# Three moves in a fused attention and MLP kernel: the output weight's casts in the last group, one subtraction block in the first group, and the places where x is added in memory

## The chip, the cores and the metric

The kernel runs on one core of one Trainium2 chip. The metric is the device time of one execution in microseconds (us). The time before is the median of three runs. One further execution was profiled; all instruction rows below come from it.

## What is computed

x has 2048 tokens of 576 features. All arithmetic is in f32.

```python
xn = layernorm(x)
A  = sliding_dilated_attention(xn @ wqkv) @ wo       # 32 heads of 18, 8 keys, 2 apart
h  = gelu(layernorm(x) @ w1)                         # 576 x 576
x1 = x + shift_quarters(h) @ w2                      # token shifts +1, -1, +2, -2
B  = x1 + gelu(layernorm(x1) @ w3) @ w4              # w3: 576 x 4608, w4: 4608 x 576
out = x + A + B
```

## The kernel before: tiles, groups and queues

**Split operands.** TensorE multiplies f32 data that was first rounded to its fast f32 form. So every operand is kept as a rounded high part and the low part that is left. ScalarE (ACT) writes the high part as a cast and VectorE (DVE) the low part as a subtraction. `split_w` (L199 to L201) does this for a weight: L200 is the cast on ACT, L201 the subtraction on DVE. Both engines take their instructions strictly in program order.

**Stages.** The kernel first computes q, k and v and keeps them in DRAM, then the token mixing (w1, w2) that gives x1, then the large MLP, and at the end the product with `wo` over 16 tiles of 128 tokens (L1431, L1437), which adds into the sum in `Y` and stores each tile. The attention itself runs on DVE, in slices between other work, during the MLP.

**The MLP's second part** is what the change touches. It has 24 groups, q = 0 to 23: groups 0 to 11 handle one half of the tokens (sb = 0, tiles 0 to 7 of the output), groups 12 to 23 the other half (sb = 1, tiles 8 to 15), both with the same 12 pairs of w3 columns. A group forms its hidden blocks from seven block products, P1 to P7, each of seven matmuls (L1130), in which sums and differences of the blocks of w3 and x take the place of an eighth product. Between the products stand the eight "downs" D0 to D7 (L868, twelve matmuls each) that multiply the *previous* group's hidden blocks with w4. Group 23 is followed by its own eight downs alone, and then by the `wo` tiles.

**Order.** TensorE's order in a group is written out by hand as a string (`ORDER`). At each item a small table, filled by `at(item, function)`, says which other work is issued right after that item:

```python
ORDER = "P1 D0 P2 P6 D1 P5 D2 P7 D3 P4 D4 P3 D5 D6 D7"
ORDERS = {0: "P1 P2 D0 P6 P5 P7 D1 D2 P4 D3 P3", ...}
```

**Names that the steps use:**
- `keep` (L1136) copies a product from PSUM on ACT; `z_add` (L1140) adds another product to it on DVE. In P7, `keep` empties the accumulator on which P4 goes on, so P4 waits for it.
- `gelu12` (L820, L821) and `low12` (L826) make the hidden block c12 out of P3's result: two gelus on ACT, then the low part on DVE. D0 of the next group multiplies c12.
- `combine` (L965) makes four sums and differences of the raw w3 block of the next group, on DVE. `split_s` (L970, L972 on ACT, L976 on DVE, L992, a small accumulating DMA on GpSimd's queue) then splits the result; the next group's P6 is its first reader. `split_a` uses L970 to L983 in the same manner for the blocks that need no combination.
- A down is read out of PSUM by ACT (L873 or L876). PSUM has two buffers for downs, so the down after next waits for it; for some tiles ACT also seeds the next buffer (L849).
- For the ten tiles in `YD = (1, 2, 3, 5, 7, 9, 10, 11, 13, 15)` the output sum lies in DRAM (`yd`). ACT copies the down into a staging slot and GpSimd (POOL) issues a DMA that accumulates it (L874). The final `+ x` is done for them by one more accumulating DMA each, `load_xa` (L886). The order in which POOL issues is the order of its queue; an accumulation on a tile waits until the one before it on that tile has landed.
- `load_wo` (L1166, L206) fetches the five row blocks of `wo` at the start of group 23, from SyncE's (SP's) queue; `split_wo(k)` splits block k into `Wo`. `read_xo` (L174) fetches the attention output behind it, `split_x` (L181 to L188) splits that, and `load_y` (L1392) fetches the `yd` sums at the end.
- `load_pair` (L954, L957) fetches the raw w3 block of a later group.

Of the kernel before, what the change touches and what calls it, by code (L numbers as in the profile page):

```python
# [33 lines left out]
YD = (1, 2, 3, 5, 7, 9, 10, 11, 13, 15)  # L34
# [3 lines left out]
NWP = NF // 2 - NPL  # L38
# [19 lines left out]
def fused_block(ctx, tc, x, wqkv, wo, w1, w2, w3, w4, out):  # L58
# [448 lines left out]
    for b in range(NB):  # L507
        for i, m in enumerate((0, 1, 2, 4, 3) if b < 3 else (4, 0, 1, 2, 3)):
# [12 lines left out]
            k = {(0, 4): 0, (1, 1): 1, (1, 4): 2, (2, 1): 3, (2, 4): 4}.get((b, i))  # L521
# [102 lines left out]
    for t in range(NT):  # L624
# [19 lines left out]
        if t in (4, 5):  # L644
            r0, c0, n = ((256, 128, 128), (HF + 256, 0, 256))[t - 4]
# [8 lines left out]
        if t in (9, 10, 13, 14):  # L654
            k = {9: 4, 10: 6, 13: 8, 14: 10}[t]
# [168 lines left out]
    def low_part(h, g):  # L824
        spent[0] += 0.69
        dve.tensor_tensor(h[:, 1, :], g, h[:, 0, :].bitcast(F32), op=ALU.subtract)  # L826
# [182 lines left out]
    for u, (c, b) in enumerate(units):  # L1009
# [77 lines left out]
        k = u % 4  # L1087
# [107 lines left out]
    for q in range(NQ):  # L1195
        sb = q // NWP
# [28 lines left out]
        low12 = lambda: low_part(hid[q, "c12"], Z2)  # L1225
        n = q + 1
        plan = {}

        def at(it, f, *args):
            plan.setdefault(it, []).append(lambda: f(*args))  # L1230

        if q == 0:
            at("P6", split_op, 0, "T4")
            at("D1", gelu22)
            at("P7", split_a, n, (0, 1))
            at("D1", split_op, 0, "B22")
            at("D1", split_a, n, (2,))
            at("D2", low22)
            at("P4", combine, n)
            at("P3", gelu12)  # L1240
            at("P3", split_s, n, (0, 1))
            at("P3", low12)
            at("P3", split_s, n, (2,))
            at("P3", load_pair, q + 2)
        elif q == NWP - 1:
            rtemps[:] = [2, 13]
            at("P1", load_w4, p, 1)
            for it, k in zip(("P1", "P2", "P6", "P5", "P7", "P4", "P3"),
                             ("B11", "B21", "T2", "T1", "T3", "T4", "B22")):
                at(it, get_op, 1, k)  # L1250
            at("P4", split_w4, p)
            at("P3", split_op, 1, "B11", 0)
            at("D2", split_op, 1, "B11", 1)
            at("D3", gelu22)
            at("D4", low22)
            at("D4", split_op, 1, "B21", 0)
            at("D5", gelu12)
            at("D5", split_op, 1, "B21", 1)
            at("D6", low12)
            at("D6", split_op, 1, "T2", 0)  # L1260
            at("D7", split_op, 1, "T2", 1)
        elif q == NWP:
            rtemps[:] = [2]
            at("D0", split_op, 1, "T1", 0)
            at("D1", split_op, 1, "T1", 1)
            at("P1", split_op, 1, "T3", 0)
            at("D2", split_op, 1, "T3", 1)
            at("P2", split_op, 1, "T4", 0)
            at("P6", split_op, 1, "T4", 1)
            at("D3", split_op, 1, "B22", 0)  # L1270
            at("P5", split_op, 1, "B22", 1)
            at("P5", split_a, n, (0, 1))
            at("P7", split_a, n, (2,))
            at("P7", combine, n)
            at("D4", gelu22)
            at("P4", low22)
            at("D5", gelu12)
            at("D5", split_s, n, (0, 1))
            at("D6", low12)
            at("D6", split_s, n, (2,))  # L1280
            at("D7", load_pair, q + 2)
        elif z < -1:
            at("P1", load_w4, p, 1)
            at("P5" if q < NWP else "D2", split_a, n, (0, 1))
            at("D2" if q < NWP else "P7", split_a, n, (2,))
            at("D3", combine, n)
            at("P4", gelu22)
            at("D4", split_w4, p, 0)
            at("D4", low22)
            at("D5", split_w4, p, 1)  # L1290
            at("P3", split_s, n, (0, 1))
            at("D5", gelu12)
            at("D5", split_s, n, (2,))
            at("D6", low12)
            if z < -2:
                at("D6", load_pair, q + 2 + (q == NWP - 2))
        else:
            at("D3", split_w4, p)
            at("P4", gelu22)
            at("D4", low22)  # L1300
            at("D5", gelu12)
            at("D6", low12)
            for k, it in enumerate(("D1", "P5", "D2", "P7", "D4")):
                at(it, split_wo, k)
        if -5 <= z <= -2:
            for i, (it, nx) in enumerate((("P6", "D1"), ("P7", "D3"), ("P3", "D5"), ("D6", "D7"))):
# [6 lines left out]
            at("D5" if q else "P3", load_w4, NPL + pair(q + 1), 0)  # L1313
        if 0 < q < 9:
            at("D6", sums, 1, q - 1)
        if 0 < q <= len(YD):
            at("D7", load_xa, YD[q - 1])
        if -4 <= z < -1:
            at("P1", put_o, z + 4)
        if z == -2:  # L1320
# [149 lines left out]
```

## Time and profile before

| | us |
|---|---|
| median of 3 runs | 1285.62 (1284.66 to 1286.82) |
| the profiled execution | 1286.14 |
| span of its instructions | 1284.3 |
| TensorE (PE) busy | 1263.6 |
| VectorE (DVE) busy | 900.2 |
| ScalarE (ACT) busy | 721.2 |
| GpSimd (POOL) busy | 252.8 |
| mean granted TensorE clock | 0.994 |

The span runs from the first to the last instruction; 1.84 us of the profiled execution lie around it. In timeline rows the columns are: start, duration, engine, line, operation, output<-input, shapes, count, and in brackets how long the engine had been idle and what released it. PEld is TensorE's weight load. SPq and POOLq rows are a queue's issues. Rows of a stretch give, for each engine, busy us and instruction count, then the granted TensorE clock (1 is full), the DMA engines' busy share and GB/s.

### The profile page before, as it was taken

The numbers are of one execution on the slowest core, as the hardware profiler recorded it, in microseconds if no ns is written. First come the engines' busy times: TensorE is split into PE (matmuls) and PEld (weight loads), VectorE is DVE, ScalarE is ACT, GpSimd is POOL, SyncE is SP. The second block draws the span as 40 slices with busy tenths as digits, with TensorE's granted clock in tenths as the row PEclk, the third lists the DMA queues.
The fourth block names the chain that finished last, engine by engine and source line by source line (L and its number), as shares of the span: only waits on it lengthen the run. The fifth ranks groups of instructions, "written<-read, shape, count | busy, mean of one in ns | idle before, by whom it ended". The sixth has DMA issues, their size and how long they took to land.

```text
span 1284.3 us, 19963 instructions
## 1 busy us (share of the span) xinstructions
PE 1263.6 (98%) x7510; PEld 1158.5 (90%) x7510; DVE 900.2 (70%) x1203; ACT 721.2 (56%) x1155; POOL 252.8 (20%) x366
## 2 busy tenths in 40 slices
PE   9999999999999999999899999999999999999799
PEld 8999998899898989999799999999888988999798
DVE  6455534778558989997659898899889973653341
ACT  3332125526645645455767768776677776775630
POOL 2011100021222111111222232232122222222100
PEclk9999999999999999999999999999999999999899
DMA  7646784246888986859679998899867678899872
GB/s 206 154 123 138 168 175 140 83 130 195 204 224 188 220 167 125 176 117 242 119 166 192 206 189 193 205 187 227 217 126 149 125 147 174 180 219 222 212 239 84
DMA packets 203800, 223.25 MB, mean 174 GB/s; under 512 B 79528, under 2 KB 139528, under 8 KB 203576
## 3 DMA queue, kind: packets, MB, share of 16 engines
q1 hardware_dynamic: 170952, 155.18, 42.4%
q0 software_dynamic: 32752, 66.80, 32.6%
q8 instruction: 59, 0.97, 0.3%
q14 instruction: 37, 0.30, 0.1%
HBM read 124.47 MB, written 107.87 MB: 181 GB/s over the span
## 4 chain that ended last, share of the span: by engine, by line
PE 60%; DMA 4%; ACT 3%; DVE 2%; issue 1%; SPq 1%; DVEq 0%; ACTq 0%; POOLq 0%
PE ps L868 29%; PE cc L1130 17%; PE p L832 10%; PE ps L215 4%; DMA w3st<-in_B_w_dram 1%; DMA x1n<-xn 1%; DMA xt<-xn 1%; DMA wr<-in_A_wo_dram 1%; DMA xt<-td1T 0%; SPq L169 0%; DMA x1n<-td1T 0%; DVE xt L597 0%; DVE w3st L965 0%; SPq L1178 0%; ACT Y L873 0%
## 5 line engine op out<-in xcount | busy, mean ns | idle before, releaser
L868 PEld LDWEIGHTS ps<-w,c 128*128 128x128 f32 x3456 | 477.5, 189 | 23.0 <-ACT c L820 3.5
L868 PE MATMUL ps<-w,c 128*128 128x288 f32 x3456 | 488.8, 295 | 6.3 <-ACT c L820 3.1
L874 POOL DMA_DIRECT2D yd<-Y x154 | 139.3, 908 | 388.2 <-ACT Y L873 330.9
L826 DVE TENSOR_TENSOR c<-Y,c 128x512 fp32r<-128x512 f32 x144 | 98.8, 687 | 93.0 <-ACT Y L815 88.0
L873 ACT COPY Y<-ps 128x576 f32<-128x576 f32 x154 | 97.9, 636 | 74.7 <-PE ps L868 62.0
L215 PE MATMUL ps<-WQ,xt 128*128 128x432 f32 x672 | 134.8, 360 | 0.0
L215 PEld LDWEIGHTS ps<-WQ,xt 128*128 128x128 f32 x672 | 125.6, 188 | 5.7
L1130 PE MATMUL cc<-xt,w3s 128*128 128x512 f32 (+1 forms) x504 | 128.0, 394 | 1.0 <-DVE Y L1140 1.0
L1130 PEld LDWEIGHTS cc<-xt,w3s 128*128 128x128 f32 (+1 forms) x504 | 92.3, 188 | 19.2 <-DVE Y L1140 1.4
L876 ACT COPY Y<-ps 128x576 f32<-128x576 f32 x92 | 58.9, 640 | 65.7 <-PE ps L868 64.3
L1130 PE MATMUL cc<-x1n,w3a 128*128 128x512 f32 (+1 forms) x336 | 86.1, 395 | 0.1
L746 DVE TENSOR_TENSOR po<-q,k 128x1152 f32<-128x1152 f32 (+1 forms) x48 | 84.2, 1755 | 0.8
L749 DVE TENSOR_REDUCE L<-po 128x64 f32<-128x1152 f32 (+1 forms) x48 | 84.0, 1751 | 0.8
L122 POOL TENSOR_TENSOR rs<-rs,mhalf 128x1 f32<-128x1 f32 x48 | 30.8, 643 | 258.0 <-DVE rs L121 147.9
L324 ACT COPY stg<-ps 128x864 f32<-128x864 f32 x24 | 21.2, 882 | 102.7 <-PE ps L215 60.4
L814 ACT ACTIVATE c<-p 128x512 fp32r<-128x512 f32 x48 | 28.6, 596 | 85.8 <-PE p L832 85.8
L722 DVE TENSOR_TENSOR po<-v,L 128x1152 f32<-128x1152 f32 x56 | 75.4, 1354 | 0.9
L1140 DVE TENSOR_TENSOR Y<-cc,Y 128x512 f32<-128x512 f32 x49 | 33.7, 687 | 53.5 <-ACT Y L1136 48.7
L1130 PEld LDWEIGHTS cc<-x1n,w3a 128*128 128x128 f32 (+1 forms) x336 | 60.7, 189 | 11.4 <-DVE w3a L976 0.4
L726 DVE TENSOR_TENSOR po<-po 128x1152 f32<-128x1152 f32 x49 | 66.4, 1355 | 0.9
L849 ACT COPY ps<-Y 128x576 f32<-128x576 f32 x92 | 59.4, 646 | 4.4 <-DVE Y L879 2.4
L215 PE MATMUL ps<-W,h 128*128 128x288 f32 x384 | 53.5, 295 | 0.0
(192 smaller groups left out, 1956.0 us busy)
## 6 DMA issues: line engine op xcount, KB each, us to landing
yd<-Y POOLq DMA_DIRECT2D x156, 288.0 KB, 6.0
Y<-in_B_w_dram SPq DMA_DIRECT2D x29, 576.0 KB, 6.0
w3st<-in_B_w_dram SPq DMA_DIRECT2D x56, 256.0 KB, 7.8
qkvd<-stg SPq DMA_DIRECT2D x24, 432.0 KB, 3.8
yd<-ev POOLq DMA_DIRECT2D x26, 288.0 KB, 7.1
w3st<-in_B_w_dram SPq DMA_DIRECT2D x92, 64.0 KB, 7.3
xd<-st SPq DMA_DIRECT2D x16, 320.0 KB, 6.1
xd<-big SPq DMA_DIRECT2D x16, 320.0 KB, 6.5
```

Of the source, the lines that this page charges most:

```text
L215: pe.matmul(ps[:, h, :n], xs(a), ws(b, h), start=i == 0, stop=i == len(PAIRS) - 1)
L722: dve.tensor_tensor(dst, vv, Lf[:, :, w:w + 1].to_broadcast([128, TPP * GH, HD]), op=ALU.mult)
L726: dve.tensor_tensor(o, o, dst, op=ALU.add)
L746: dve.tensor_tensor(dst, qf[:, None, :].to_broadcast([128, n, TPP * GC]), win, op=ALU.mult)
L749: dve.tensor_reduce(Lw[:, w:w + n, :], dst.rearrange("p w (x d) -> p w x d", d=HD), axis=AX.X, op=ALU.add)
L826: dve.tensor_tensor(h[:, 1, :], g, h[:, 0, :].bitcast(F32), op=ALU.subtract)
L832: pe.matmul(ps, W3[f][:, w, :], x1n[b][:, a, :], start=n == 0, stop=n == len(PAIRS) - 1)
L849: act.copy(ps[:, :, :HF], halves(t))
L868: pe.matmul(ps[:, k, :HF], h[:, col], w[:, p, k * HF:(k + 1) * HF], start=n == 0 and not seed, stop=n == len(seq) - 1, skip_group_check=True)
L873: act.copy(e.rearrange("p (h c) -> p h c", h=2), ps[:, :, :HF])
L874: pool.dma_start(yd[t], e, accum_op=ALU.add)
L1130: pe.matmul(ps, WX[w][:k, v, SLOT[w], :], area[sb][xk][:k, a, :], start=onto is None and i == 0, stop=last and i == len(HALVES) - 1, skip_ ...
```

## The change

```diff
         if q == 0:
...
             at("D2", low22)
-            at("P4", combine, n)
             at("P3", gelu12)
+            at("P3", combine, n)
+            at("P3", low12)
             at("P3", split_s, n, (0, 1))
-            at("P3", low12)
             at("P3", split_s, n, (2,))
...
             at("D6", low12)
-            for k, it in enumerate(("D1", "P5", "D2", "P7", "D4")):
+            for k, it in enumerate(("P4", "D4", "P3", "D5", "D6")):
                 at(it, split_wo, k)
...
-        if 0 < q <= len(YD):
-            at("D7", load_xa, YD[q - 1])
+        if 0 < q - sb * NWP <= 5:
+            at("D7", load_xa, YD[5 - 5 * sb + q - sb * NWP - 1])
```

**First group (q = 0).** `combine` goes from behind P4 to behind P3 and its `z_add`. These are DVE's rows around the end of group 0, before; `cc` is a product, `c` a hidden block, `w3st` the raw w3 block:

```order
L826 TENSOR_TENSOR c_5906<-Y,c_5906 128x512
L965 TENSOR_TENSOR w3st<-w3st 128x3x128 x4
L1140 TENSOR_TENSOR Y<-cc_5866,Y 128x512
L826 TENSOR_TENSOR c_5965<-Y,c_5965 128x512
L976 TENSOR_TENSOR w3s<-w3st,w3s 128x1024
```

And the same place on DVE now:

```order
L826 TENSOR_TENSOR c_5906<-Y,c_5906 128x512
L1140 TENSOR_TENSOR Y<-cc_5866,Y 128x512
L965 TENSOR_TENSOR w3st<-w3st 128x3x128 x4
L826 TENSOR_TENSOR c_5961<-Y,c_5961 128x512
L976 TENSOR_TENSOR w3s<-w3st,w3s 128x1024
```

The four subtractions and additions of L965 have changed places with the addition of L1140. They still stand ahead of c12's low part (the second L826) and of `split_s`.

**Last group (q = 23).** The five casts of `wo` leave the items D1, P5, D2, P7 and D4 and go to P4, D4, P3, D5 and D6. These are ACT's rows from D1's copy on, before:

```order
L873 COPY Y<-ps_11148 128x576
L200 CAST Wo<-wr 128x576 x2
L876 COPY Y<-ps_11199 128x576
L849 COPY ps_11266<-Y 128x2x288
L200 CAST Wo<-wr 128x576
L1136 COPY Y<-cc_11172 128x512
L200 CAST Wo<-wr 128x576
L873 COPY Y<-ps_11236 128x576
L569 CAST w_11149<-Y 128x2x576
L820 ACTIVATE c_11305<-Y 128x512
L821 ACTIVATE Y<-Y 128x512
L876 COPY Y<-ps_11266 128x576
```

ACT's rows now, from the same copy on:

```order
L873 COPY Y<-ps_11148 128x576
L876 COPY Y<-ps_11199 128x576
L849 COPY ps_11262<-Y 128x2x288
L1136 COPY Y<-cc_11172 128x512
L873 COPY Y<-ps_11236 128x576
L569 CAST w_11149<-Y 128x2x576
L820 ACTIVATE c_11297<-Y 128x512
L821 ACTIVATE Y<-Y 128x512
L200 CAST Wo<-wr 128x576
L876 COPY Y<-ps_11262 128x576
L200 CAST Wo<-wr 128x576 x2
L873 COPY Y<-ps_11287 128x576
```

P7's `keep` (L1136) had three casts between itself and D1's copy, and now has none; the first cast stands eight rows later. The fourth cast now stands behind `gelu12`, and the fifth behind the seed (L849) for the first down of the last eight. DVE's L201 rows move along.

**x added in memory.** Before, groups 1 to 10 each added x to one tile of `YD` in its order; that is tiles 1, 2, 3, 5, 7 in groups 1 to 5, while these groups' own downs accumulate on the same tiles, and 9, 10, 11, 13, 15 in groups 6 to 10. Now groups 1 to 5 add x to tiles 9, 10, 11, 13, 15, groups 6 to 10 to none, and groups 13 to 17 to tiles 1, 2, 3, 5, 7. On POOL's queue, around the downs of groups 13 and 14, these rows stand now (the number behind `yd` is the tile):

```order
L874 DMA yd9_92<-Y_71 128x576
L874 DMA yd10_93<-Y_71 128x576
L874 DMA yd11_94<-Y_71 128x576
L886 DMA yd1_87<-in_A_x_dram 128x576
L874 DMA yd13_95<-Y_71 128x576
L983 DMA w3a_9097<-w3t_86 32x384
L874 DMA yd15_96<-Y_71 128x576
```

Before, the same stretch of the queue had no L886 row:

```order
L874 DMA yd9_92<-Y_71 128x576
L874 DMA yd10_93<-Y_71 128x576
L874 DMA yd11_94<-Y_71 128x576
L874 DMA yd13_95<-Y_71 128x576
L983 DMA w3a_9101<-w3t_86 32x384
L874 DMA yd15_96<-Y_71 128x576
```

So one accumulating DMA has come in behind the eighth down, ahead of the next group's first staged tile. The count of instructions is the same on every engine.

## The prediction

> **What bounds the kernel now.** The page first: which engine is nearest to the whole span?
>
> ```profile
> span 1284.3 us, 19963 instructions
> PE 1263.6 (98%) x7510; PEld 1158.5 (90%) x7510; DVE 900.2 (70%) x1203; ACT 721.2 (56%) x1155; POOL 252.8 (20%) x366
> ```
>
> TensorE is idle for 1284.3 - 1263.6 = 20.7 us. The change removes no matmul, so it can only win idle time, and time in which TensorE runs at a low clock. Next, TensorE's waits, longest first, and two rows of the view by stretches:
>
> ```profile
> PE cc L1130 <- ACT Y L1136: 6.9, 2, 6.6
> PE ps L868 <- ACT c L820: 3.1, 1, 3.1
> ...
> 935.00:1160.00 225.00, 225.00 (x1342) 203.26 (x1341) 156.88 (x193) 158.59 (x251) 54.50 (x64) 1.00 0.80 165
> 1160.00:1220.00 60.00, 52.50 (x317) 48.12 (x316) 23.01 (x33) 37.61 (x60) 11.30 (x14) 0.91 0.91 209
> ```
>
> One wait of 6.6 us (a product for the copy of L1136) and one of 3.1 us (a down for the gelu of L820) make half of the idle time. From 935 to 1160 us TensorE has no idle time at all; in the 60 us from 1160 it loses 7.5 us, and its granted clock sinks to 0.91. The change works in both waits, so I read their stretches in the timeline and the chain of waits.
>
> **The last group.** Rows of the timeline and, for the load, the units of 1.59 and 1.62 us and the last line, of the chain:
>
> ```profile
> 1141.73 1.59 PE ps L868 x12
> 1143.32 1.62 PE cc L1130 x7
> ...
> 1183.81 7.50 DMA wr<-in_A_wo_dram
> ...
> 1185.09 1.78 PE L1130 MATMUL cc<-x1n,w3s 128*128 128x512 f32 x7
> ...
> 1191.41 1.28 ACT L200 CAST Wo<-wr 128x576 fp32r<-128x576 f32 x2 [8.69 <-DMA wr<-in_A_wo_dram]
> 1195.04 3.35 PE L1130 MATMUL cc<-xt,w3a 128*128 128x512 f32 x7 [6.58 <-ACT Y L1136]
> 1204.55 0.64 ACT L873 COPY Y<-ps 128x576 f32<-128x576 f32 x1 [2.03 <-PE ps L868]
> 1206.94 0.64 ACT L849 COPY ps<-Y 128x576 f32<-128x576 f32 x1
> 1207.64 4.92 PEld L868 LDWEIGHTS ps<-w,c 128*128 128x128 f32 x36 [0.19 <-ACT ps L849]
> 1209.58 0.64 ACT L876 COPY Y<-ps 128x576 f32<-128x576 f32 x1 [0.23 <-PE ps L868]
> 1213.04 0.63 ACT L873 COPY Y<-ps 128x576 f32<-128x576 f32 x1
> 1213.72 8.20 PE ps L868 x60
> ```
>
> The reader is to see a queue blocked by a load. The first block of `wo` lands at 1183.81 + 7.50 = 1191.31. Its cast (L200, 1191.41) stands on ACT right behind D1's copy. Behind it stand D2's copy, the seed, and L1136, for which P4 waits. So P4 starts at 1195.04.
>
> *P4 without the casts ahead.* P7 starts at 1185.09, D3 behind it; P4 can start at 1185.09 + 1.62 + 1.59 = 1188.30, which is 6.74 us earlier. L1136 is free to run at P7's end, 1186.87, since nothing on ACT is then waiting for memory.
>
> *From P4 to the fourth of the last eight downs.* Before, this stretch is 1213.72 - 1195.04 = 18.68 us. It holds two products and seven downs, at full clock 2 x 1.62 + 7 x 1.59 = 14.37 us. The other 4.31 us are half clock (P4 took 3.35 us instead of 1.62, and the down behind it was slow too) and short waits for ACT. With the idle time gone the clock has no reason to fall, but ACT now has the casts in this stretch, and I count them. The first cast comes at about 1191.4, behind `gelu22`, when its block has just landed; D4's copy stands behind it and has until 1194.7. D5's copy can start at P4 + 1.62 + 1.59 + 1.62 + 1.75 = 1194.9. From D5's copy to the seed of the last eight's first down ACT takes 1206.94 - 1204.55 = 2.39 us; the fourth cast adds 1.28 / 2 = 0.64, so the seed starts at 1197.95 and the down 0.70 later (1207.64 - 1206.94), at 1198.65. TensorE would be ready at 1188.30 + 2 x 1.62 + 4 x 1.59 = 1197.90: 0.75 us lost. The fifth cast and two gelus delay this down's copy by about 0.2 us, to 1200.6. From that copy to the fourth down the first part of `split_x` stands on ACT, as before: 1213.72 - 1209.58 = 4.14. So the fourth down starts at 1204.7 instead of 1213.72. **Term 1: -9.0 us.** From there the instructions and their order are as before; the casts are over by 1199.1 and their DVE parts soon after, more than 12 us ahead of the first `wo` tile.
>
> **The first group.** Timeline rows from c22's low part to P6 of group 1, with the landing time of all L992 DMAs below, and TensorE's clock in one of those microseconds:
>
> ```profile
> 634.00 2.33 DVE L965 TENSOR_TENSOR w3st<-w3st 128x384 f32<-128x384 f32 x4
> 636.25 0.68 DVE L1140 TENSOR_TENSOR Y<-cc,Y 128x512 f32<-128x512 f32 x1
> 637.65 1.04 PE L868 MATMUL ps<-w,c 128*128 128x288 f32 x4 [3.11 <-ACT c L820]
> 638.17 1.03 ACT L970 CAST w3s<-w3st 128x1024 fp32r<-128x1024 f32 x1
> 638.29 0.69 DVE L826 TENSOR_TENSOR c<-Y,c 128x512 fp32r<-128x512 f32 x1 [1.36 <-ACT Y L821]
> 639.04 2.29 PE L868 MATMUL ps<-w,c 128*128 128x288 f32 x8 [0.35 <-DVE c L826]
> 640.12 0.77 POOL L992 DMA_DIRECT2D w3s<-w3st  x1 [4.12 <-ACT w3s L972]
> 642.66 0.42 PEld L1130 LDWEIGHTS cc<-xt,w3s 128*128 128x128 f32 x2
> ...
> DMA to landing us min/median/max: 2.4/2.5/5.2
> ...
> 639.00:640.00 1.00, 0.96 (x4) 0.96 (x5) 0.77 (x1) 1.00 (x3) 0.00 (x0) 0.50 0.08 16
> ```
>
> With the places exchanged, L1140 starts at 634.00, 2.25 us earlier, and D0 can begin 637.65 - 2.25 = 635.40. But c12's low part (L826) still stands behind L965, which now ends at about 634.00 + 0.68 + 2.25 = 636.93 (the lengths from start to start): the low part goes from 638.29 to 636.95, 1.34 us earlier, and D0 halts for it after four matmuls. `split_s` (L970) also needs L965: 638.17 becomes 636.97, 1.2 us earlier, and with it L992's DMA: 640.12 becomes 638.92. Before, that DMA (2.5 us) landed at 642.6 and P6 read it at 642.66, with no slack. So P6 moves by 1.2 us, however early D0 is. **Term 2: -1.2 us** (bounds: -0.8, if TensorE stays at half clock and is itself late for P6; -1.9, the most that D0 and P2 allow).
>
> The row of 639 us shows half clock after a wait of 3.1 us. The Trainium skill ("TensorE: Matmul & The Clock Gate", "Part 1: The HAM clock gate") says that the clock is halved after an idle window of about 3.4 us. By that rule two gaps of 0.9 and 1.0 us with work between keep full clock; by the row, where less sufficed, part of the half clock may stay, which is the end at -0.8.
>
> **x added elsewhere.** Rows: POOL's waits, two rows of group 7, two of group 14, then the landing times of w3's blocks (L954) before and after 880 us, and of the x adds:
>
> ```profile
> POOL yd L886 <- DMA yd<-Y: 10.2, 2, 7.3
> ...
> 818.34 0.84 ACT L970 CAST w3a<-w3st 128x768 fp32r<-128x768 f32 x1 [2.98 <-DMA w3st<-in_B_w_dram]
> 821.45 1.87 PE L1130 MATMUL cc<-xt,w3a 128*128 128x512 f32 x7 [0.35 <-ACT Y L1136]
> 980.45 0.90 SPq L954 DMA_DIRECT2D w3st<-in_B_w_dram  x2
> 992.19 0.83 ACT L970 CAST w3a<-w3st 128x768 fp32r<-128x768 f32 x1
> ...
> DMA to landing us min/median/max: 2.7/7.6/11.3
> ...
> DMA to landing us min/median/max: 5.8/8.5/9.5
> ...
> DMA to landing us min/median/max: 4.0/6.2/9.7
> ```
>
> In groups 1 to 5 the adds waited on POOL for the tile's own accumulation, 10.2 us in two of them. TensorE had no idle time there, so their end is worth nothing: the staging slots hide it. Groups 6 to 10 lose an add each. One stall lies there: in group 7 a w3 block landed late, ACT waited 2.98 us and P4 0.35, and P4 ran 0.24 us long (1.86 is its length after a wait, 1.62 without). Without the add beside that load I take the stall as gone: **-0.6** (bounds 0 and -1.5, since the transition at 870 to 935 us has 2 us of idle time, mostly DVE's). Groups 13 to 17 gain an add each. There a w3 block is issued at 980.45 and used at 992.19: 11.7 us, against landings of at most 9.5 without adds and of 11.3 in the first half with them. No stall would follow; I charge **+0.3** (bounds 0 and +3).
>
> **Sum.** -9.0 - 1.2 - 0.6 + 0.3 = -10.5 us. The profiled execution took 1286.14, so 1275.6; the median of the runs, 0.52 below it, would give 1275.1. I take 1275.4.
>
> **Rivals.**
>
> *The tail becomes memory's (slower than forecast, still faster than before).*
>
> ```profile
> 1208.77 0.87 POOL L874 DMA_DIRECT2D yd<-Y  x1 [0.57 <-ACT Y L873]
> 1216.22 1.24 SPq L174 DMA_DIRECT2D x1n<-xd  x2
> 1233.88 0.75 DVE L1431 TENSOR_TENSOR Y<-ps,Y 128x576 f32<-128x576 f32 x1
> 1236.55 14.97 PE L215 MATMUL ps<-Wo,xt 128*128 128x288 f32 x112
> ```
>
> The third block of the attention output is fetched at 1216.22, when the accumulation issued at 1208.77 has landed (`load_y` waits for its slot). The second `wo` tile's addition waits on DVE behind that block's split, at 1233.88, and the fifth tile (1236.55) needs the buffer that it frees: 1.9 us of slack. When TensorE is 9 us earlier, the accumulations of D5 to D7 fall among the reads of the first two blocks, and may land 2 to 4 us later than their new places ask for. That takes 0 to 3 us back: 1276 to 1279. For it speaks the small slack; against it that the loads are all started by TensorE's progress and so move along.
>
> *The casts still wait (the change does not do what it says).* If the `wo` blocks land 4 us later than 1191.3, the first cast holds D4's copy, which has 2 to 3 us to spare. This gives back the rest and adds short waits: 1277 to 1281. Nothing in the change delays these loads.
>
> *The added x adds starve groups 13 to 17 (slower than before).* Place: the w3 block of the next group, whose cast stands on ACT ahead of the copy that P4 waits for. Price: five times the lateness. It decides from 10.5 / 5 = 2.1 us per group, a landing 13.8 us after issue, since 11.7 are allowed; at 3 us each the time is 1275.4 + 15 = 1290. The add takes 6.2 us; sharing all engines evenly it could add some 3 us to a landing of 9.5, which gives 0.8 us a group, 1279 in all. Against more speaks the first half: with adds and other accumulations no load took over 11.3 us. The Trainium skill ("DMA: Bandwidth & Descriptors", "Queues, rings and completion order") says that each DMA engine takes turns between the queues that have work, packet by packet. By that rule an add can stretch a load by its own 6.2 us at most, to 15.7, 4 us late in each group and 1295.
>
> **Chances.** Forecast (1273 to 1278) 0.66; memory in the tail (to 1280) 0.18; casts that wait 0.06; starved groups, slower than before, 0.05; a mixture that ends near the old time, 0.05, of which I put 0.03 within 0.2% (2.6 us, about what a measurement of this kernel can tell from no change) and 0.02 above. So faster 0.90, same 0.03, slower 0.07. The range: at the low end all favourable bounds, -9.2 - 1.9 - 1.5 = -12.6 from 1285.6, 1273.0; at the high end 3 us given back in the tail, -0.8 in the first group and +1.5 in groups 13 to 17, net -5.3, 1280.5.
>
> **What would show it.** In the changed profile: P4 of the last group at P7 + 3.2 us with no wait for L1136, and no half clock there. A wait of under 1 us at the first and about 1.2 us at the fourth of the last eight downs. In group 1, two short waits of D0 in place of one, P6 1.2 us earlier. No wait in group 7, and L970 in groups 13 to 17 not released by a DMA. I am wrong if the tail of L215 has new waits for L1431, or if casts L200 are released by `wr` at a time when copies stand behind them.

## The result, and the profile after

The changed kernel took 1276.7 us (median of 6 runs, 1275.16 to 1279.68) against 1285.45 us for the kernel before, measured beside it (6 runs, 1284.66 to 1286.82): ratio 0.9935, 95% interval 0.9919 to 0.995. That is faster by about 8.4 us, more than the 0.2% that can be told from no change. It was run twice more, with medians of 1275.63 and 1275.67; over all 17 runs the median is also 1275.63. The forecast was 1275.4.

The profiled execution of the changed kernel is the slowest of its first six, 1279.68 us. Its page begins:

```profile
span 1277.8 us, 19971 instructions
PE 1261.6 (99%) x7510; PEld 1155.8 (90%) x7510; DVE 900.3 (70%) x1203; ACT 722.2 (57%) x1155; POOL 253.0 (20%) x366
```

TensorE's idle time is 1277.8 - 1261.6 = 16.2 us, 4.5 less than before. The span is 6.5 us shorter, though, and TensorE's busy time fell by 2.0 us with the same 7510 matmuls: that part is half clock that has gone. Where the idle time is now, longest waits first (in us: total, times, longest):

```profile
PE ps L868 <- ACT Y L873: 2.1, 2, 1.2
PE ps L868 <- DVE c L826: 1.4, 1, 1.4
...
PE cc L1130 <- ACT cc L1333: 1.4, 2, 1.1
...
PE ps L868 <- ACT c L820: 0.9, 1, 0.9
```

The wait of 6.6 us for L1136 and that of 3.1 us for L820 are both gone. What is left are short waits for low parts (L826), for the copy of a product that stands behind `split_s` on ACT (L1333), for gelus and for copies. The stretches, with the granted clock and the DMA share behind the engines' busy times:

```profile
935.00:1160.00 225.00, 224.99 (x1341) 203.13 (x1340) 157.57 (x193) 160.06 (x255) 59.00 (x69) 1.00 0.83 169
1162.00:1222.00 60.00, 58.08 (x381) 54.21 (x381) 26.80 (x37) 41.98 (x66) 13.75 (x16) 1.00 0.98 241
```

In groups 13 to 21 TensorE still has no idle time, with the five x adds of groups 13 to 17 among them (POOL has 69 rows instead of 64). The last 60 us before the `wo` tiles lose 1.9 us of TensorE instead of 7.5, at full clock instead of 0.91. Now the last group in the timeline of the changed kernel, from P7 to the fourth of the last eight downs:

```profile
1187.43 1.79 PE L1130 MATMUL cc<-x1n,w3s 128*128 128x512 f32 x7
1189.25 0.59 ACT L1136 COPY Y<-cc 128x512 f32<-128x512 f32 x1 [0.25 <-PE cc L1130]
1190.64 1.79 PE L1130 MATMUL cc<-xt,w3a 128*128 128x512 f32 x7
...
1194.56 0.68 ACT L200 CAST Wo<-wr 128x576 fp32r<-128x576 f32 x1 [0.82 <-DMA wr<-in_A_wo_dram]
1195.67 1.25 ACT L200 CAST Wo<-wr 128x576 fp32r<-128x576 f32 x2
1199.13 0.66 ACT L200 CAST Wo<-wr 128x576 fp32r<-128x576 f32 x1
1200.36 0.64 ACT L849 COPY ps<-Y 128x576 f32<-128x576 f32 x1
1201.05 5.19 PE L868 MATMUL ps<-w,c 128*128 128x288 f32 x36 [0.65 <-ACT ps L849]
1207.16 1.06 PE L868 MATMUL ps<-w,c 128*128 128x288 f32 x6 [0.92 <-ACT Y L873]
```

L1136 runs right at P7's end, and P4 starts 1190.64 - 1187.43 = 3.21 us after P7 with no wait. The first cast still waits 0.82 us for its block, but a copy behind it has time to spare. Two waits remain, 0.65 us for the seed of the first of the last eight downs and 0.92 us for a copy ahead of the fourth.

To compare executions whose starts differ, I use the time between the starts of the same TensorE matmuls, from the PE rows of each profile: G1 is group 1 from the last matmul of its first product (P1) to the first of D1; G8 is group 8 from P7 to the end of P4, the place of the stall that the prediction puts in group 7 (counted from q = 0, as in `ORDERS`, P7 at 817.7 us of the kernel before belongs to group 8); G13-21 lies between the same two matmuls near 934 and 1152 us, from group 13 into group 22; T1 runs from P7 to P4 of the last group, T2 from P4 to D5, T3 from D5 to the fourth of the last eight downs, T4 from there to the first `wo` tile. All in us:

| kernel profiled | G1 | G8 | G13-21 | T1 | T2 | T3 | T4 |
|---|---|---|---|---|---|---|---|
| before | 10.37 | 5.43 | 217.55 | 9.95 | 7.72 | 10.96 | 8.03 |
| changed (first profile) | 9.99 | 4.84 | 217.71 | 3.21 | 4.84 | 11.68 | 8.04 |
| changed (after_again) | 9.62 | 4.84 | 217.73 | 3.21 | 4.84 | 11.55 | 8.03 |
| changed (after_side) | 8.40 | 4.84 | 217.75 | 3.21 | 4.84 | 11.56 | 8.04 |
| casts_only | 11.63 | 4.93 | 217.65 | 3.21 | 4.84 | 11.55 | 8.03 |
| combine_only | 8.41 | 5.68 | 217.56 | 12.01 | 6.61 | 10.96 | 8.03 |
| adds_only | 10.62 | 4.84 | 217.56 | 10.16 | 6.36 | 10.95 | 8.03 |
| no_adds | 9.28 | 5.66 | 217.55 | 3.21 | 4.84 | 11.55 | 8.03 |
| first_at_D2 | 9.35 | 4.84 | 217.60 | 6.95 | 6.46 | 11.54 | 8.03 |
| first_at_P7 | 8.41 | 4.84 | 217.54 | 3.21 | 4.84 | 13.55 | 8.03 |
| low_first | 13.24 | 4.84 | 217.54 | 3.21 | 4.84 | 11.55 | 8.03 |
| last_two_later | 9.23 | 4.84 | 218.58 | 3.21 | 4.84 | 11.09 | 8.04 |
| last_two_side | 10.65 | 4.84 | 217.55 | 3.21 | 4.84 | 10.96 | 8.03 |
| split_spread | 9.47 | 4.84 | 217.55 | 3.21 | 4.84 | 11.15 | 8.61 |

T1 to T3 together fell from 28.63 to 19.73 us in the first profile, 8.9 us, G8 by 0.6, and G1 by 0.4 there and by 2.0 in another. The theory is the prediction's: the casts are the main term, because of what stood behind them on ACT's queue, not because of their work. The rivals to tell apart: the gain comes in part from the other two edits; or the casts' ACT time is what counts, wherever they stand; or a wait moves to the `wo` tiles.

### The profile page after: what moved, and what is told of

The parts are those of the page before. It is cut to its first block, busy times and chain, and to the rows that moved or that the text cites. A ratio compares the mean times of both kernels' runs of the same rounds, so it can differ in the third digit from the quotient of the medians.

```text
span 1277.8 us, 19971 instructions
## 1 busy us (share of the span) xinstructions
PE 1261.6 (99%) x7510; PEld 1155.8 (90%) x7510; DVE 900.3 (70%) x1203; ACT 722.2 (57%) x1155; POOL 253.0 (20%) x366
## 4 chain that ended last, share of the span: by engine, by line
PE 63%; DMA 3%; ACT 2%; DVE 2%; issue 1%; SPq 0%; DVEq 0%; ACTq 0%
PE ps L868 30%; PE cc L1130 19%; PE p L832 10%; PE ps L215 4%; DMA w3st<-in_B_w_dram 1%; DMA xt<-xn 1%; DVE w3st L965 1%; DMA x1n<-td1T 0%; DVE xt L597 0%; SPq L1178 0%; DMA Y<-od 0%; PE p L1437 0%; ACT Y L873 0%; ACT xt L927 0%; DVE w3a L976 0%
## 5 line engine op out<-in xcount | busy, mean ns | idle before, releaser
L826 DVE TENSOR_TENSOR c<-Y,c 128x512 fp32r<-128x512 f32 x144 | 98.8, 687 | 88.9 <-ACT Y L815 87.4
L873 ACT COPY Y<-ps 128x576 f32<-128x576 f32 x154 | 98.1, 637 | 75.2 <-PE ps L868 61.7
L876 ACT COPY Y<-ps 128x576 f32<-128x576 f32 x92 | 59.0, 641 | 65.6 <-PE ps L868 64.2
L814 ACT ACTIVATE c<-p 128x512 fp32r<-128x512 f32 x48 | 28.7, 599 | 85.7 <-PE p L832 85.7
L1140 DVE TENSOR_TENSOR Y<-cc,Y 128x512 f32<-128x512 f32 x49 | 33.7, 688 | 59.9 <-ACT Y L1136 55.1
L849 ACT COPY ps<-Y 128x576 f32<-128x576 f32 x92 | 59.4, 645 | 4.4 <-DVE Y L879 2.4
```

The lines of the kernel that those rows point to most:

```text
L849: act.copy(ps[:, :, :HF], halves(t))
L873: act.copy(e.rearrange("p (h c) -> p h c", h=2), ps[:, :, :HF])
```

## Experiments: one part at a time

Four kernels ran side by side: the kernel before with each part of the change alone, and the changed kernel again. The kernel before took 1286.06 us there (21 runs).

**casts_only** is the kernel before with this line alone:

```diff
-            for k, it in enumerate(("D1", "P5", "D2", "P7", "D4")):
+            for k, it in enumerate(("P4", "D4", "P3", "D5", "D6")):
```

> Only the casts of wo move; first group and x adds as before. Theory A (each part pays for itself, by the sum): -9.0 us, so about 1276.4 against 1285.4, P4 of the last group at P7 + 3.2 us without a wait, 0.7 us lost at the first and 1.2 us at the fourth of the last eight downs. Theory B (memory: the casts only pay because the x adds no longer crowd the queues and wo lands earlier): clearly less than -9, about -6. Theory C (it is the first group that pays most): about -3.

Measured: 1278.3 us (5 runs, 1275.88 to 1278.86), ratio 0.993 (0.9916 to 0.9944). T1 to T3 are those of the changed kernel to 0.13 us. So this one line makes the whole gain of the last group. Its median is 7.8 us below before rather than 9.0; its own profile lost 1.3 us in group 1 (G1 11.63) and 1.5 us in group 7 (25.55 us from its P1 to the next, against 24.06 before), whose code it does not touch.

**combine_only** is the kernel before with the order at group 0's P3:

```diff
-            at("P4", combine, n)
             at("P3", gelu12)
+            at("P3", combine, n)
+            at("P3", low12)
             at("P3", split_s, n, (0, 1))
-            at("P3", low12)
             at("P3", split_s, n, (2,))
```

> Only the subtraction block of the first group moves. Theory A: -1.2 us, 1284.2, if TensorE keeps full clock in group 1, and -0.3 if the half clock only moves from D0 to P2 and P6, as in the profile of the changed kernel (their fourteen matmuls took 5.07 us instead of 3.23). In the profile D0 begins 2.1 us earlier and goes on 1.3 us earlier either way. Theory C (the whole wait of 3.1 us goes): -3.

Measured: 1285.43 us (11 runs, 1283.61 to 1287.88), ratio 0.9993 (0.9983 to 1.0003): no difference that can be told. Yet its profile shows G1 at 8.41 instead of 10.37, 2.0 us won. Group 1 and the last group in its timeline:

```profile
636.03 0.80 PE L868 MATMUL ps<-w,c 128*128 128x288 f32 x4 [0.86 <-ACT c L820]
...
638.22 1.32 PE L868 MATMUL ps<-w,c 128*128 128x288 f32 x8 [1.39 <-DVE c L826]
...
639.22 0.58 ACT L1333 COPY cc<-cc 128x512 f32<-128x512 f32 x1
639.62 0.77 POOL L992 DMA_DIRECT2D w3s<-w3st  x1 [2.98 <-PE ps L868]
639.85 1.89 PE L1130 MATMUL cc<-x1n,w3a 128*128 128x512 f32 x7 [0.31 <-ACT cc L1333]
641.57 1.77 PE L1130 MATMUL cc<-xt,w3s 128*128 128x512 f32 x7
...
1183.55 1.79 PE L1130 MATMUL cc<-x1n,w3s 128*128 128x512 f32 x7
...
1191.56 0.67 ACT L200 CAST Wo<-wr 128x576 fp32r<-128x576 f32 x1 [10.38 <-DMA wr<-in_A_wo_dram]
1195.56 3.36 PE L1130 MATMUL cc<-xt,w3a 128*128 128x512 f32 x7 [8.64 <-ACT Y L1136]
```

P7 of the last group starts at 1183.55, 1.54 us earlier than before, and the cast of the first `wo` block at 1191.56, against 1191.41 before. So P4 waits 8.64 us where it waited 6.58. That load was issued 1.2 us earlier, too, but took 8.8 us instead of 7.5 to land. T1 to T3 together are 29.58 us instead of 28.63, so in this execution the last group took back 1.0 of the 1.5 us. That it must do so is not shown: in all 14 profiles the load is issued 0.9 to 2.3 us ahead of P7, so it comes earlier with whatever is won ahead of it, and its landing time alone runs from 5.0 to 8.8 us.

**adds_only** is the kernel before with the x adds moved:

```diff
-        if 0 < q <= len(YD):
-            at("D7", load_xa, YD[q - 1])
+        if 0 < q - sb * NWP <= 5:
+            at("D7", load_xa, YD[5 - 5 * sb + q - sb * NWP - 1])
```

> Only the x adds change groups. Theory A: -0.3 us, between -1.5 and +3, not to be told from no change; group 7's wait of 0.35 us goes, groups 13 to 17 get no wait on w3's blocks. Theory B (memory): -2 to -4 us, and wo's first block lands earlier than 7.5 us after its issue.

Measured: 1286.75 us (11 runs, 1283.54 to 1288.48), ratio 0.9998 (0.9987 to 1.0008): no difference that can be told. G8 is 4.84 instead of 5.43, the 0.6 us of the prediction, and groups 13 to 21 are as before. The wait of the last group is longer than before here too, though T1 to T3 together, 27.47 us, are 1.2 us shorter, as the clock was at half for a shorter time behind it:

```profile
1196.56 3.32 PE L1130 MATMUL cc<-xt,w3a 128*128 128x512 f32 x7 [6.78 <-ACT Y L1136]
```

**after_again** is the changed kernel.

> The changed kernel itself, on the same chip as its parts. Theory A: the parts add up, about -10, 1275 to 1276, and single runs spread by 2 to 4 us, since the profiled one lost 2.2 us between 319 and 345 us, where nothing was changed. Theory B or C: the parts do not add up.

Measured: 1275.63 us (5 runs, 1274.45 to 1278.66), ratio 0.9919 (0.9903 to 0.9936). By the medians the three parts alone give -7.8, -0.6 and +0.7 us, -7.7 in sum; together -10.4. By the ratios they add up: 0.9930, 0.9993 and 0.9998 make 0.9921 for the sum, against 0.9919 measured, and the two small parts are worth some 1.2 us alone and 1.4 us behind the casts. With intervals of 0.0010 to 0.0017 to either side neither reading can be told from the other, so the runs do not show that the small parts are worth more once the casts have moved.

## Experiments: queue order or ACT's work

Beside these kernels the kernel before took 1287.06 us (12 runs). In each kernel one entry or one order of the changed kernel is different.

**first_at_D2** puts only the first cast back, ahead of L1136 on ACT's queue:

```diff
-            for k, it in enumerate(("P4", "D4", "P3", "D5", "D6")):
+            for k, it in enumerate(("D2", "D4", "P3", "D5", "D6")):
```

> The changed kernel with only the first of the five casts put back, from P4 to D2, so that it stands between D2's copy and P7's keep (L1136). Theory A (what cost time was L1136 queued behind a cast that waits for its block): P4 waits until the block has landed, some 4 us, with half clock behind it, so 4 to 6 us slower than the changed kernel, near 1281. Rival (the casts' own work, 3.2 us of ACT, was too much at that place): one cast of 0.64 us moves, so within 1 us of the changed kernel.

Measured: 1282.95 us (5 runs, 1278.45 to 1285.46), ratio 0.9966 (0.995 to 0.9983). ACT's work is the same 0.67 us, at another place of the queue. Its timeline:

```profile
1185.28 1.79 PE L1130 MATMUL cc<-x1n,w3s 128*128 128x512 f32 x7
...
1191.02 0.67 ACT L200 CAST Wo<-wr 128x576 fp32r<-128x576 f32 x1 [4.17 <-DMA wr<-in_A_wo_dram]
1191.60 0.58 ACT L1136 COPY Y<-cc 128x512 f32<-128x512 f32 x1
1192.23 2.85 PE L1130 MATMUL cc<-xt,w3a 128*128 128x512 f32 x7 [3.58 <-ACT Y L1136]
```

ACT waits 4.17 us for the block, L1136 stands behind it, P4 waits 3.58 us and then runs 2.85 us instead of 1.79. T1 to T3 are 24.95 us against 19.60 in the profile of after_again: one cast of 0.67 us at this place costs 5.4 us, more than half of the 8.9 us that the change won here. It is the order of the queue that counts.

**first_at_P7** puts the first cast right behind L1136 instead:

```diff
-            for k, it in enumerate(("P4", "D4", "P3", "D5", "D6")):
+            for k, it in enumerate(("P7", "D4", "P3", "D5", "D6")):
```

> The changed kernel with the first cast moved from P4 to P7, right behind L1136 and ahead of D3's copy. Theory A: P4 does not wait; the cast still waits for its block and holds D3's copy, which D5 needs only 3.5 to 4 us later; the copies behind it are late by 1 to 3 us, so the time is 1 to 2.5 us above the changed kernel. Rival (any cast ahead of P4 costs as much): as in the run with the cast at D2.

Measured: 1278.4 us (4 runs, 1277.8 to 1279.85), ratio 0.9934 (0.9922 to 0.9947). Its timeline:

```profile
1185.34 0.59 ACT L1136 COPY Y<-cc 128x512 f32<-128x512 f32 x1 [0.25 <-PE cc L1130]
1186.73 1.78 PE L1130 MATMUL cc<-xt,w3a 128*128 128x512 f32 x7
...
1189.91 0.67 ACT L200 CAST Wo<-wr 128x576 fp32r<-128x576 f32 x1 [3.98 <-DMA wr<-in_A_wo_dram]
...
1199.02 5.18 PE L868 MATMUL ps<-w,c 128*128 128x288 f32 x36 [1.52 <-ACT ps L849]
```

The cast waits 3.98 us for its block, as long as in first_at_D2, and P4 no longer cares. What is late now is the chain of copies behind it: the seed L849 makes the first of the last eight downs wait 1.52 us instead of 0.65, and T3 is 13.55, 2.0 us above the changed kernel's. A second wait, 0.63 us for a copy (L876) ahead of this, belongs to the same chain. One place on ACT's queue, ahead of L1136 or right behind it, decides between 5.4 and 2.0 us.

**low_first** takes the low part ahead of `combine` in group 0, for the claim that P6 is held by `split_s`'s DMA whatever D0 does:

```diff
             at("P3", gelu12)
-            at("P3", combine, n)
             at("P3", low12)
+            at("P3", combine, n)
             at("P3", split_s, n, (0, 1))
```

> The changed kernel with low12 ahead of combine at P3 of the first group. Theory A (P6 waits for the small DMA of split_s, so D0's own speed is worth nothing): D0 runs through without its wait of 1.4 us for the low part, L992 is issued some 0.7 us later, P6 starts 0.3 to 0.7 us later than in the changed kernel, and the whole time is within 1 us of it. Rival (D0's second wait is time lost): 1 to 1.4 us faster than the changed kernel.

Measured: 1279.88 us (5 runs, 1278.8 to 1280.89), ratio 0.9944 (0.9932 to 0.9956): slower than the changed kernel's three medians by 3.2 to 4.3 us. Its timeline in group 1:

```profile
636.81 2.01 PE L868 MATMUL ps<-w,c 128*128 128x288 f32 x8 [0.59 <-DVE c L826]
...
639.08 1.04 ACT L970 CAST w3s<-w3st 128x1024 fp32r<-128x1024 f32 x1 [3.05 <-DVE w3st L965]
...
640.65 0.57 ACT L1333 COPY cc<-cc 128x512 f32<-128x512 f32 x1
...
641.28 3.35 PE L1130 MATMUL cc<-x1n,w3a 128*128 128x512 f32 x7 [2.46 <-ACT cc L1333]
```

D0 has only a short halt, as meant. But the copy of P1 (L1333) stands on ACT behind the `split_s` rows, which wait for L965, and P2 waits 2.46 us for it. I had missed this wait; it is the one that holds group 1. Part of the loss is clock: it was at half for 10.2 us here, against 3.4 us in the changed kernel's first profile.

**last_two_later** takes the last two casts out of D5 and D6, to behind the fourth and fifth of the last eight downs, for the 0.65 us left at the first:

```diff
-            for k, it in enumerate(("P4", "D4", "P3", "D5", "D6")):
+            for k, it in enumerate(("P4", "D4", "P3")):
...
+        if j in (3, 4):
+            split_wo(j)
```

> The changed kernel with the fourth and fifth casts moved on, behind the fourth and fifth of the last eight downs. Theory A (the fourth cast delays the seed of the first of these downs, 0.6 us of wait in the profile): that wait goes, 0.5 to 1 us faster than the changed kernel, 1275 or just below. Rival (ACT has no room there, so that the casts delay the copies of later downs instead): no change or slower.

Measured: 1276.39 us (6 runs, 1275.18 to 1279.22), ratio 0.9923 (0.991 to 0.9936). T3 falls to 11.09, as thought, but the time cannot be told from the changed kernel's, which did not run beside it.

## Experiments: is there a better version, and what are the adds worth?

Beside these kernels the kernel before took 1287.1 us (11 runs). **after_side** is the changed kernel, **last_two_side** the kernel of last_two_later.

> The changed kernel, to stand on the same chip beside the three others of this call. Both theories: ratio to before near 0.992, with single profiles that spread by some 3 us.

> The fourth and fifth casts behind downs 4 and 5 of the last eight, again, beside the changed kernel. Its profile had gained 1.0 us at the first of these downs. Theory A: 0.5 to 1 us faster than the changed kernel. Rival: the same, because something later takes the gain.

Measured: 1275.67 us (6 runs, 1274.88 to 1279.36), ratio 0.9923 (0.9908 to 0.9938), against 1276.33 (5 runs, 1275.68 to 1276.99), ratio 0.9923 (0.9909 to 0.9936). T3 is 11.56 and 10.96: the 0.6 us is gone in the trace, and the time does not show it; with intervals of some 1.8 us to either side it could not.

**no_adds** is the changed kernel with the x adds back in groups 1 to 10 (the reverse of the diff of adds_only).

> The changed kernel with the x adds put back to groups 1 to 10. Theory A (adds are hidden either way): within 1 us of the changed kernel. Theory B (with the casts gone, memory decides, and the adds' move is worth something): 1 to 3 us slower than the changed kernel.

Measured: 1276.4 us (5 runs, 1276.0 to 1276.73), ratio 0.9923 (0.9908 to 0.9938): not to be told from the changed kernel. Its timeline shows the stall of group 8 back:

```profile
817.60 0.83 ACT L970 CAST w3a<-w3st 128x768 fp32r<-128x768 f32 x1 [3.20 <-DMA w3st<-in_B_w_dram]
...
820.72 1.88 PE L1130 MATMUL cc<-xt,w3a 128*128 128x512 f32 x7 [0.58 <-ACT Y L1136]
```

**split_spread** is last_two_later with the first `split_x` spread over the first, second and fourth of the last eight downs (`split_x` gets a parameter `piece` for it) and the last two casts moved one down further, so that fewer long ACT rows stand together:

```diff
-        if j in (0, 2):
-            split_x(xo[0], j // 2)
+        if j < 2:
+            split_x(xo[0], 0, piece=j)
+        if j == 3:
+            split_x(xo[0], 1)
+        if j in (4, 5):
+            split_wo(j - 1)
```

> As before this one, and the first split of the attention output is spread: its two 64-row casts stay behind the first of the last eight downs, the others go behind the second and the fourth, and the casts of wo behind the fifth and sixth. Theory A: the wait of about 1 us at the fourth of these downs shrinks to 0.3 or less, so 1.5 to 2 us faster than the changed kernel. Rival: the copies behind the moved casts are late instead, no gain.

Measured: 1276.21 us (5 runs, 1275.5 to 1277.36), ratio 0.9922 (0.9908 to 0.9936), the same again. Its lines are numbered two higher, so that L875 is the L873 of the others. The wait at the fourth of the last eight downs has not gone:

```profile
1203.59 0.64 ACT L875 COPY Y<-ps 128x576 f32<-128x576 f32 x1 [1.03 <-DMA yd<-Y]
...
1204.28 1.85 PE L870 MATMUL ps<-w,c 128*128 128x288 f32 x12 [1.11 <-ACT Y L875]
```

It is 1.11 us instead of 0.92, since the copy now waits 1.03 us for an accumulation to land (by its output a staging slot's) and not for a cast. A wait of 0.31 us for a seed follows, and T4 is 8.61 instead of 8.03.

So no version was found that beats the changed kernel.

## Why the prediction was right, point by point

**Term 1, the casts: -9.0 us predicted, -8.9 to -9.0 in the stages.** T1 fell by 6.74 us, as worked out; T2 by 2.88, the half clock and P4's slow run; and T3 rose by 0.6 to 0.7, the wait for the seed of the first of the last eight downs (0.65 us, forecast 0.75). The size hangs on the execution that one starts from: the three profiles with the casts in their old places took 27.47, 28.63 and 29.58 us for T1 to T3. casts_only shows the term by itself, first_at_D2 that it is the place in ACT's queue.

**Term 2, the combine: -1.2 us predicted; G1 gave -0.4 to -2.0.** D0's and the low part's new times were right (in combine_only, whose group 0 starts 0.63 us later than before, 636.03 and 638.22 for D0's two halves). This step failed: "Before, that DMA (2.5 us) landed at 642.6 and P6 read it at 642.66, with no slack. So P6 moves by 1.2 us, however early D0 is." In combine_only the DMA was issued at 639.62 and P6 started at 641.57, less than 2.5 us later; this landing time, from the view of that line there:

```profile
DMA to landing us min/median/max: 2.5/2.5/2.5
```

So P6's first matmuls do not read what it brings, and it did not hold them. The kernel says why: by `HALVES` the seven matmuls of a product take slots 3, 1, 3, 4, 2, 4 and 0 of `w3s`, and the DMA of `split_s` fills slot 0, which only the seventh reads. In each of the 14 profiles it had landed 0.8 us or more ahead of that matmul. What holds is P2, 0.31 us in combine_only, by L1333 behind `split_s` on ACT; low_first made this wait 2.46 us and lost what it had meant to win. TensorE's rows of the changed kernel's first profile:

```profile
637.76 0.80 PE L868 MATMUL ps<-w,c 128*128 128x288 f32 x4 [0.87 <-ACT c L820]
...
639.95 1.32 PE L868 MATMUL ps<-w,c 128*128 128x288 f32 x8 [1.39 <-DVE c L826]
...
641.58 3.05 PE L1130 MATMUL cc<-x1n,w3a 128*128 128x512 f32 x7 [0.31 <-ACT cc L1333]
```

The waits here are those of combine_only, 0.87, 1.39 and 0.31 us, but P2 runs 3.05 us instead of 1.89. The rest of the spread is clock, which the last section explains. In the ten profiles with `combine` moved (low_first left out) G1 is 9.28 us on average, in the three without it, before among them, 10.87: -1.6 us. Sorted by the clock, the ten have 8.40 to 8.41 us with no stretch of 3.4 us at half clock there, 9.23 to 9.99 with one and 10.65 with two; the three have 10.37 and 10.62 with one and 11.63 with two. So at equal clock the move is worth 1.0 us, and the rest is fewer stretches at half clock. The value taken, -1.2, was a fair middle for a wrong reason, and so partly luck.

**Term 3, x added elsewhere: -0.6 + 0.3 predicted.** G8 is 4.84 in all ten profiles with the adds moved, and 5.43, 4.93, 5.68 and 5.66 in the four without: -0.6 on average. A stall of this kind is not tied to that place, nor to an add, however. In low_first, which has the adds moved, it stands in group 7:

```profile
797.86 0.83 ACT L970 CAST w3a<-w3st 128x768 fp32r<-128x768 f32 x1 [2.83 <-DMA w3st<-in_B_w_dram]
...
800.97 1.89 PE L1130 MATMUL cc<-xt,w3a 128*128 128x512 f32 x7 [1.03 <-ACT Y L1136]
```

Groups 2 to 10 as a whole took 216.54 to 217.84 us in the ten profiles and 217.13 to 218.28 in the four, -0.7 on average: the size held, and that the add beside the load is the cause is not shown. Groups 13 to 17 alone took 121.98 to 122.17 us with the adds and 122.00 in all four without, less than +0.1 on average rather than +0.3. (The 218.58 in one row of the table is a wait of 0.8 us in group 21.) The w3 blocks issued there (932 to 1062 us of the changed kernel) landed so, against 5.8/8.5/9.5 before:

```profile
DMA to landing us min/median/max: 6.1/8.5/9.9
```

The longest landing grew by 0.4 us here; over all profiles it is 9.9 to 11.0 us with the adds and 9.2 to 10.1 without, some 1 us more, and 11.7 are allowed. In time by itself the part is too small to be measured (adds_only and no_adds).

**The rivals.** The tail did not become memory's: T4 and the `wo` tiles behind it are as long as before, and the tail's chain is one run of matmuls.

```profile
1215.36 55.52 PE ps L215 x420
```

The casts did still wait, 0.82 us in the changed kernel's first profile, which cost next to nothing at the new places (T3 is 11.68 there and 11.55 in the next); first_at_P7 shows what a wait of 3.98 us would have cost, 2.0 us. The starved groups did not come. The Trainium skill ("DMA: Bandwidth & Descriptors", "Queues, rings and completion order") says that each DMA engine takes turns between the queues that have work. By that the prediction let an add stretch a load by up to its own 6.2 us; the runs show some 1 us at the longest landing.

**Slips that do not touch the forecast.** The low end of the range takes -9.2 for a term that stands as -9.0, and its high end, -5.3 from 1285.6, is 1280.3 and not 1280.5. The groups of the rows from 817 us on are numbered one too low: the stall lies in group 8, and the load issued at 980.45 in group 15.

**What the forecast left out.** The 17 runs of the changed kernel lie in two clusters, ten from 1274.45 to 1275.82 and seven from 1277.91 to 1279.68. Part of that is a stretch that the change does not touch, the timeline of the changed kernel's first profile around 317 us:

```profile
316.70 0.63 ACT L606 ACTIVATE xt<-xt 64x512 fp32r<-64x512 f32 x1 [4.29 <-DMA xt<-xn]
...
321.08 3.29 PE L832 MATMUL p<-xt,w3a 128*128 128x512 f32 x13 [1.08 <-ACT Y L815]
```

And the row of before that answers to its first:

```profile
314.45 0.63 ACT L606 ACTIVATE xt<-xt 64x512 fp32r<-64x512 f32 x1 [2.32 <-DMA xt<-xn]
```

The load of `xt` lands 2.2 us later. Between the same two matmuls, at 318.5 and 345.0 us of the kernel before, the profiles take either 26.5 to 27.4 us (eleven of them, before among them) or 28.7 to 28.9 (the first profile, after_again and first_at_D2). The two profiles of the changed kernel in the upper cluster, 1279.68 and 1278.18, have the late load, and the one in the lower, 1275.82, has not. Half of the first six runs lie in the upper cluster and two of the five and of the six later ones, which is why the first median, 1276.7, lies above the forecast and the two later ones on it. That the other runs of the upper cluster had the late load too is likely and not shown, since one execution of each set was profiled; and why the load is late in some executions stays open.

## What to carry to other kernels

On an engine that works in order, price an instruction that waits for memory by what stands behind it in the queue, and not by its length: a cast of 0.67 us cost 5.4 us in front of a copy that TensorE needed, 2.0 us right behind it, and 0.6 to 0.7, with the four others, from five rows behind it on. Small gains cannot be added up from medians that spread by more than the gain: compare the stages of the traces, and at equal clock. And when a step is to be held by a transfer, check in the trace that the first instruction reads what it brings, and list every copy that stands on the same queue behind the moved rows.

## What the runs showed of the hardware

The half clock after a short wait is no fixed price; it depends on where the wait falls. TensorE's granted clock moves on a fixed grid: in each of the 14 profiles all its changes lie whole multiples of 3.413 us apart, and where the grid starts differs from execution to execution. The changed kernel's first profile in group 1, cut along its grid (busy TensorE time behind the length, the clock third from the end):

```profile
635.13:638.54 3.41, 2.51 (x11) 1.61 (x10) 3.34 (x7) 2.46 (x4) 0.87 (x1) 1.00 0.00 0
638.54:641.95 3.41, 1.72 (x11) 1.42 (x11) 2.54 (x4) 2.58 (x5) 0.61 (x1) 1.00 0.73 91
641.95:645.37 3.42, 3.42 (x10) 2.66 (x9) 0.69 (x1) 2.45 (x6) 0.17 (x1) 0.50 0.28 29
```

And combine_only, with gaps of the same size, along its own grid:

```profile
636.04:639.45 3.41, 2.02 (x12) 1.64 (x12) 2.78 (x5) 2.41 (x4) 0.60 (x1) 1.00 0.66 83
639.45:642.87 3.42, 3.11 (x14) 2.51 (x14) 1.19 (x2) 3.39 (x7) 0.77 (x1) 1.00 0.23 27
```

In the first, the gaps of 1.39 and 0.31 us fall into one stretch, which is idle for 1.69 of its 3.41 us, and the next stretch runs at half clock. In combine_only a boundary parts them, 1.39 us in one stretch and 0.31 in the next, and the clock stays full. Over all 14 profiles the 17 stretches at full clock with 1.69 us or more of idle TensorE time were each followed by one at half clock, the 5156 with less than 1.44 us by none, and of the nine between, two. So what counted here is the sum of the idle time in a stretch of the grid, with a limit near half of it (the ends of matmuls are modelled, so the limit is known to 0.1 or 0.2 us), and the price comes in whole stretches. Over group 1 the clock was at half for 0, 3.4, 6.8 or 10.2 us: not at all in combine_only, 3.4 us in the kernel before, 6.8 in casts_only and 10.2 in low_first.

The Trainium skill ("TensorE: Matmul & The Clock Gate", "Part 1: The HAM clock gate") says that a free-running window of some 3.4 us decides on the clock; the grid agrees with it. Its condition, a whole idle window, does not hold here: no gap in group 1 of the changed kernel's first profile was longer than 1.4 us, and half of a window sufficed.
